# A fused recurrence, gated convolution and MLP on one core: two full rings of raw q/k/f tiles, a third activation buffer, three weights loaded in column halves, state copies on either of two engines, and another search for the order of the units

## The chip, the core and the metric

The kernel runs on one core of a Trainium2 chip. The metric is the device time of one execution in microseconds (us). TensorE (PE in the rows) does the matrix products and the transposes by an identity, VectorE (DVE), ScalarE (ACT) and GpSimd (POOL) the elementwise work, and SyncE (SP) issues every transfer. Each engine works through its own list of instructions in the order in which the program holds them.

## What is computed

All inputs are float32 numbers in four batches of 768 tokens; the weights come as float64 words and are turned into float32 on the chip. A recurrence per head gives y, a gated convolution with two products follows, and then a normalised two-layer MLP with a residual:

```python
def _attn_ref(q, k, v, f_logit):                     # 4 batches, 8 heads, 768 tokens, 48 wide
    f = 1.0 / (1.0 + np.exp(-f_logit))
    for t in range(S):
        state = f[:, :, t, :, None] * state + np.einsum('bhd,bhe->bhde', k[:, :, t], v[:, :, t])
        y[:, :, t] = np.einsum('bhd,bhde->bhe', q[:, :, t], state)

def _moe_ref(x, w_val, conv_w, w_out):               # x: 768 tokens x 384; conv_w: 5 x 384
    for k in range(K):
        gate_pre += conv_w[k][None, None, :] * xp[:, k:k + S, :]
    gate = 1.0 / (1.0 + np.exp(-gate_pre))
    return (gate * (x @ w_val) @ w_out)

def _moe2_ref(x, g_ln, w_ch1, w_ch2):                # w_ch1: 384 x 1536, w_ch2: 1536 x 384
    xn = (x - mu) / np.sqrt(var + 1e-06) * g_ln
    return x + np.maximum(xn @ w_ch1, 0.0) @ w_ch2
```

## The kernel before, in words

**Tiles and stages.** The 3072 tokens are worked in 24 tiles of 128 tokens, and two tiles make one of 12 groups of 256. A tile goes through the recurrence in chunks of 64 tokens: `load` and `load_v` bring q, k, f and v, `prep` turns f, k and q so that the channel lies on the partitions (`turned`) and makes the decays, scaled keys `kt` and scaled queries `mv` on DVE, `at_t` turns `kt` (PE block T) and copies it to `kn` on ACT, `at_a` makes the products inside a chunk (block A), `at_d` the state (block D, then `sd` on POOL, the copies `st<-sd` on ACT and `sn` on DVE), `at_y` the outputs (block Y) and copies them to `xt`, six small transfers on SP moving the last 16 rows of each head. A group then goes through `gates` (a product and four multiply-adds per 128 channels, the multiply-adds on DVE, and a sigmoid), `val` (27 matmuls on `wv`, `gt`), `x1` (18 on `wo`, then mean and variance, `rs` and `nb` on POOL, `xn` on ACT and its product with `gln`), `xnt` (the transposes `ps<-ident,xn`) and 6 steps of `c1` (18 matmuls and the relu) and `c2` (12 matmuls). Every product of these is done three times on parts: each operand is split into a high part `hi` and a rest `lo` of type float32r (`split`, `mm3`). The relu of `c1` leaves `hidden_hi` (ACT) and `hidden_lo` (DVE), which `c2` reads, from a ring of two buffers.

**The raw tiles.** The first eight tiles (`TURNED`) are loaded as they lie and turned by PE; from the ninth on they are loaded in four pieces and turned by DVE (`dve_transpose`). There is one set of full buffers `raw_f`, `raw_k`, `raw_q`, and a smaller set `odd_*` that only the odd ones of the first eight tiles use. `load(a + 1)` is written behind `prep(a)`.

**The weights.** They come through `stage`, four slots of 384 words of 8 bytes; `w_val` and `w_out` fill three slots each with transfers that cover 48 and 16 partitions (`ROWS`), `w_ch1` and `w_ch2` fill one slot at a time. `convert` puts a float32 together from the two halves of a float64 in four instructions for 128x384 words: one on POOL or ACT (`scaled`), one on ACT or DVE (`shifted`), one on ACT (`REBIAS`), one on DVE; `split` then makes `w_hi` (ACT or DVE) and `w_lo` (POOL or DVE).

**What sets the order.** The program is first recorded as units with their dependencies and a price on each engine that may do them; a planner (`schedule`, `pass_over`) then walks through them in modelled time, always taking the unit that can start first, by rank among equals. It also chooses the engine where there is a choice (`side` is POOL or DVE, `mover` ACT or DVE, `scaler` POOL or ACT; `BIAS` is added to DVE's side) and the PSUM bank of each result (8 banks, `ps`). 120 passes are made with ranks from a backward pass or with random shifts, and the one with the shortest modelled span is issued by `emit`, so that nearly every instruction has the line of one call in it (L413 before, L466 after). Groups 0 and 1 share the first halves of the MLP, so that each weight is used for both: steps 1 to 12 of `c1` belong to these two groups, the 13th opens group 2.

Of the kernel before, what the change touches and what calls it, by code (L numbers as in the profile page):

```python
# [21 lines left out]
DM = H * D  # L22
# [12 lines left out]
KS = 5  # L35
EPS = 1e-6
MIN_DECAY = 1e-15
PASSES = 120
ALTERNATE = 8
SPREADS = (0.5, 2.0, 6.0)  # L40
SEED = 1
# [4 lines left out]
load6 gates1 v5 w  # L46
# [5 lines left out]
BIAS = 0.9  # L52
# [8 lines left out]
SLOTS = 4  # L61

# [32 lines left out]
class Unit:  # L95


    def __init__(self, engine):
        self.costs = dict.fromkeys(engine.split("|"), 0.0)
        self.engine = next(iter(self.costs))  # L100
        self.calls = []
        self.delay = 0.0
        self.deps = set()
        self.opens = None
        self.uses = set()
        self.port = False
# [13 lines left out]
class Plan:  # L120
# [111 lines left out]
    def price(self, engine, method, out, ins, n, args, kw):  # L232
        if engine == "tensor":
            if method == "transpose":
                return 0.105 * self.slow
            if ins[0].dtype == F32R:
                return (0.436e-3 * n + 0.006) * self.slow
            return (0.056 if n > D else 0.043) * self.slow
        if engine == "scalar":
            scaled = sum(isinstance(kw.get(k), bass.AP) for k in ("scale", "bias"))  # L240
            part = 0.1 if out.ap[0][1] < 128 else 0.0
            return n / 1200 + (0.066 if ins[0].space == PSUM else 0.096) + 0.093 * scaled + part
        if engine == "vector":
            if method == "reciprocal":
# [12 lines left out]
            return n / (1920 if fast else 960) + 0.069 + 0.062 * scalars  # L257
        if engine == "gpsimd":
            if args and args[-1] == ALU.pow:
                return 0.5  # L260
            if method == "affine_select":
                return 0.62
            if method in ("memset", "tensor_copy"):
                return 0.0009 * n + 0.07
            return (0.0029 if method in ("tensor_scalar", "scaled") else 0.0024) * n + 0.1
        raise ValueError(engine)

    def transfer(self, issued, u, out, in_):

        n = size = mybir.dt.size(out.dtype)  # L270
        for _, k in out.ap:
            n *= k
        run = size * min(out.ap[-1][1], in_.ap[-1][1])
        local = out.space == in_.space
        issued.costs = {"sync": 0.63 if out.ap[0][1] == 64 or local else 0.47}
        issued.delay = 0.5
        u.costs = {"wire": n / run * (10.0 + (0.054 if run < 1024 else 0.048 if run < 2048 else 0.064) * run) / 16e3}
        u.delay = 1.2
        u.deps.add(len(self.units) - 1)

    def wait(self, u, v):

        if u.engine != v.engine:
            after = {"tensor": 0.17, "vector": 0.085, "scalar": 0.1, "gpsimd": 0.05}
            before = {"tensor": 0.07, "gpsimd": 0.085}
            return u.delay + after.get(u.engine, 0.05) + before.get(v.engine, 0.04)
        return u.delay + {"tensor": 0.0, "vector": 0.115, "scalar": 0.12}.get(u.engine, 0.11)

    def pass_over(self, deps, users, rank, wait, forward):
# [4 lines left out]
        free, waiting = {}, {}  # L294
# [6 lines left out]
        for u in units:  # L301
            for e in u.costs:
                free[e], waiting[e] = 0.0, []

        def enter(i):
            for e in units[i].costs if forward else [units[i].engine]:
                waiting[e].append(i)

        def start(i, e):
            t = max(free[e], ready[i])  # L310
            if units[i].port and e in port:
                t = max(t, port[other[e]])
            if forward and units[i].opens is not None:
                t = max(t, min(banks.values()) if banks else 1e9)
            if forward and units[i].opens is not None and e == "vector":
                t = max(t, sorted(banks.values())[1] if len(banks) > 1 else 1e9)
            if e == "sync":
                t = max(t, free["wire"] - BACKLOG)
            return t
# [4 lines left out]
        def fits(i, e):  # L324
            costs = units[i].costs
            return len(costs) == 1 or not forward or finish(i, e) <= min(finish(i, x) for x in costs)

        for i in range(len(units)):
            if not left[i]:
                enter(i)  # L330
        order = []
        while len(order) < len(units):
            best = None
            for e, q in waiting.items():
                for i in q:
                    t = (start(i, e), rank[i])
# [3 lines left out]
            if t >= 1e9:  # L340
                return None, None, 1e9, None
            u = units[i]
            for x in u.costs if forward else [e]:
                waiting[x].remove(i)
            u.engine = e
            order.append(i)
            end[i] = free[e] = t + u.costs[e]
            if u.port and e in port:
                port[e] = end[i] + 0.05
            if forward:  # L350
                if u.opens is not None:
                    homes[u.opens] = min(banks, key=banks.get)
                    del banks[homes[u.opens]]
                for r in u.uses:
                    held[r] -= 1
                    ends[r] = max(ends[r], end[i] + 0.17)
                    if not held[r]:
                        banks[homes[r]] = ends[r]
            for j in users[i]:
                left[j] -= 1  # L360
                ready[j] = max(ready[j], end[i] + wait(u, units[j]))
                if not left[j]:
                    enter(j)
        return order, end, max(free.values()), homes

    def schedule(self):

# [6 lines left out]
        back = lambda u, v: self.wait(v, u)  # L374
        draw = random.Random(SEED)
        rank, best, kept = list(range(len(units))), None, None
        for n in range(PASSES):
            order, end, span, homes = self.pass_over(deps, users, rank, self.wait, True)
            better = best is None or span < best[1]
            if better:  # L380
                best = order, span, [u.engine for u in units], homes
                kept = rank
            if order and (n < ALTERNATE or better):
                _, end, _, _ = self.pass_over(users, deps, [-t for t in end], back, False)
                rank = [-t for t in end]
            else:
                far = draw.choice(SPREADS)
                rank = [t + draw.gauss(0.0, far) for t in kept]
        order, self.makespan, engines, homes = best
# [26 lines left out]
class Kernel:  # L416
    def __init__(self, ctx, tc, aps):
# [29 lines left out]
        self.raw = {n: one(f"raw_{n}", [128, NP, 4 * D]) for n in "fkq"}  # L447
        self.odd = {n: one(f"odd_{n}", [128, N]) for n in "fkq"}
# [26 lines left out]
        self.hidden = [parts(f"hidden{i}", [128, 2, G]) for i in range(2)]  # L475
        self.banks = ring("ps", BANKS, [128, 512], pool=ps)

    def constants(self):
        nc = self.nc
        self.ns = self.n1 = self.n2 = self.na = self.nw = self.slot = 0  # L480
        for n, pad in (("f", 8.0), ("k", 0.0), ("q", 0.0)):
            for raw in (self.raw[n], self.odd[n]):
                nc.gpsimd.memset(self.by_token(raw)[:, :, D:], pad)
            nc.gpsimd.memset(self.raw[n][:, :, 160:192], pad)
# [272 lines left out]
    def at_d(self, a):  # L757
# [16 lines left out]
        for c in range(NC):  # L774
# [8 lines left out]
            else:  # L783
# [131 lines left out]
    def c1(self, g, i):  # L915
# [10 lines left out]
        hh, hl = self.hidden[self.n1 % 2]  # L926
# [4 lines left out]
    def c2(self, g, i, stops=(NK // 2 - 1,)):  # L931

        nc = self.nc
        hid = self.hidden[self.n2 % 2]
# [34 lines left out]
    def record(self):  # L969
# [205 lines left out]
```

## Time and profile before

| | us |
|---|---|
| median of 3 runs | 556.89 (556.07 to 557.33) |
| the profiled execution | 557.31 |
| its span | 555.6 |
| PE busy | 504.9 (91%) |
| DVE busy | 349.0 (63%) |
| ACT busy | 298.3 (54%) |
| POOL busy | 189.8 (34%) |

The span is the time between the first and the last recorded work of the profiled execution; its own time is 1.7 us longer. Busy shares are means over stages that differ: at the beginning weights and eight tiles come in and are converted, in the middle one group of 256 tokens follows another, and at the end a check of the decays and the last output follow.

### The profile page before, as it was taken

Reading aid. Unit: us, or ns where it says so; the run is one execution under the profiler, and the core shown is the slowest. Engines: PE = TensorE matmul, PEld = TensorE weight load, DVE = VectorE, ACT = ScalarE, POOL = GpSimd, SP = SyncE. Lnnn points to the kernel's source line nnn. Section 1 sums busy time; section 2 is a strip of 40 time slices with the busy share of each in tenths; the row PEclk is TensorE's granted clock in tenths of the full one; section 3 lists DMA queues with packets and bytes.
Section 4 is the critical chain, followed back from the end, with each engine's and each line's share of the span. In section 5 each row is a group of like instructions: output and inputs, shape, how many; then the busy total and the mean of one; then the engine's idle time right before and its main releaser. Section 6 shows DMA issues by size and latency. Waiting matters only on the chain.

```text
span 555.6 us, 13472 instructions
## 1 busy us (share of the span) xinstructions
PE 504.9 (91%) x5272; PEld 476.2 (86%) x5272; DVE 349.0 (63%) x681; ACT 298.3 (54%) x659; POOL 189.8 (34%) x298
## 2 busy tenths in 40 slices
PE   5656859999989999989989999999999999999994
PEld 4545749889989989989989989989989999999994
DVE  8737895589986686676676676676676361362311
ACT  4848999995464464464464464464463472421310
POOL 2433578763340341340440441430430541411200
PEclk9965979999999999999999999999999999999998
DMA  7996766542732332242232242242220010000000
GB/s 140 171 164 157 178 162 198 154 132 47 180 94 59 81 102 54 69 103 58 63 106 56 64 115 58 53 117 56 53 66 15 14 32 9 8 31 1 28 1 34
DMA packets 92128, 45.60 MB, mean 82 GB/s; under 512 B 56213, under 2 KB 89749, under 8 KB 92058
## 3 DMA queue, kind: packets, MB, share of 16 engines
q1 hardware_dynamic: 92058, 44.67, 34.3%
q8 instruction: 43, 0.70, 0.5%
q14 instruction: 27, 0.22, 0.1%
HBM read 38.75 MB, written 4.72 MB: 78 GB/s over the span
## 4 chain that ended last, share of the span: by engine, by line
PE 61%; ACT 14%; DVE 11%; DMA 5%; issue 4%; SPq 2%; POOL 2%; DVEq 0%; ACTq 0%; POOLq 0%
PE ps L413 61%; DVE ps L413 6%; ACT wt L413 4%; ACT ps L413 3%; DMA raw_f<-in_f_logit 3%; SPq L413 2%; DMA xt<-x 2%; ACT w_hi L413 1%; DVE x L413 1%; POOL rs L413 1%; ACT st L413 1%; ACT x L413 1%; DVE hidden_lo L413 1%; DVE ps L961 1%; ACT kn L413 1%
## 5 line engine op out<-in xcount | busy, mean ns | idle before, releaser
L413 PE MATMUL ps<-nh,w_hi 128*128 128x256 f32 x432 | 124.4, 288 | 0.2 <-ACT nh L413 0.2
L413 PE MATMUL ps<-nl,w_hi 128*128 128x256 f32 x432 | 120.5, 279 | 0.3 <-DVE nl L413 0.2
L413 PE MATMUL ps<-nh,w_lo 128*128 128x256 f32 x432 | 120.3, 279 | 0.0
L413 PE MATMUL ps<-w_hi,hidden_hi 128*128 128x384 f32 x288 | 100.8, 350 | 0.1
L413 PE MATMUL ps<-w_hi,hidden_lo 128*128 128x384 f32 x288 | 97.1, 337 | 0.1
L413 DVE SCALAR_TENSOR_TENSOR hidden_lo<-ps,hidden_hi 128x512 fp32r<-128x512 f32 x72 | 49.3, 685 | 76.0 <-ACT hidden_hi L413 75.9
L413 PE MATMUL ps<-w_lo,hidden_hi 128*128 128x384 f32 x288 | 96.8, 336 | 0.0
L413 PEld LDWEIGHTS ps<-nh,w_hi 128*128 128x128 f32 x432 | 81.2, 188 | 2.0 <-ACT nh L413 0.4
L413 PEld LDWEIGHTS ps<-nl,w_hi 128*128 128x128 f32 x432 | 81.2, 188 | 0.7 <-DVE nl L413 0.7
L413 PEld LDWEIGHTS ps<-nh,w_lo 128*128 128x128 f32 x432 | 81.7, 189 | 0.0
L413 ACT ACTIVATE hidden_hi<-ps 128x512 fp32r<-128x512 f32 x72 | 43.0, 597 | 59.5 <-PE ps L413 59.3
L413 DVE SCALAR_TENSOR_TENSOR ps<-xt,convw,ps 128x256 f32<-128x256 f32 x144 | 66.1, 486 | 12.5 <-ACT ps L413 10.6
L413 POOL TENSOR_TENSOR gl<-gt,gh 128x512 fp32r<-128x512 f32 (+1 forms) x24 | 24.3, 1014 | 108.5 <-ACT gh L413 108.5
L413 PEld LDWEIGHTS ps<-w_hi,hidden_hi 128*128 128x128 f32 x288 | 54.1, 188 | 2.4 <-ACT hidden_hi L413 0.4
L413 PEld LDWEIGHTS ps<-w_hi,hidden_lo 128*128 128x128 f32 x288 | 54.1, 188 | 0.5 <-DVE hidden_lo L413 0.4
L413 PEld LDWEIGHTS ps<-w_lo,hidden_hi 128*128 128x128 f32 x288 | 54.2, 188 | 0.0
L413 ACT COPY st<-sd 48x192 f32<-48x192 f32 x88 | 31.0, 353 | 40.7 <-POOL sd L413 39.3
L413 POOL TENSOR_SCALAR_AFFINE_SELECT mv<-mv 64x512 f32<-64x512 f32 x48 | 31.6, 658 | 50.5 <-ACT mv L413 48.6
L413 POOL TENSOR_TENSOR sd<-sn,fc 112x192 f32<-112x192 f32 x44 | 22.5, 510 | 55.1 <-DVE sn L413 45.7
L413 PEld LDWEIGHTS ps<-mv,st 112*48 112x48 f32 (+1 forms) x768 | 24.5, 126 | 15.4 <-ACT st L413 9.2
L413 PE MATMUL ps<-mv,st 112*48 112x64 f32 (+1 forms) x768 | 29.1, 225 | 9.0 <-ACT st L413 8.0
L413 ACT COPY kn<-ps 64x192 f32<-64x192 f32 x96 | 30.2, 315 | 9.9 <-PE ps L413 8.8
(105 smaller groups left out, 1032.4 us busy)
## 6 DMA issues: line engine op xcount, KB each, us to landing
stage<-in_moe_w_ch SPq DMA_DIRECT2D x24, 384.0 KB, 4.0
st<-in_v SPq DMA_DIRECT2D x96, 48.0 KB, 2.5
out_x<-x SPq DMA_DIRECT2D x24, 192.0 KB, 1.9
raw_f<-in_f_logit SPq DMA_DIRECT2D x32, 96.0 KB, 2.4
raw_k<-in_k SPq DMA_DIRECT2D x32, 96.0 KB, 2.2
raw_q<-in_q SPq DMA_DIRECT2D x32, 96.0 KB, 2.4
raw_f<-in_f_logit SPq DMA_DIRECT2D x32, 80.0 KB, 2.3
raw_k<-in_k SPq DMA_DIRECT2D x32, 80.0 KB, 2.2
```

Source lines behind the costliest of these rows:

```text
L413: getattr(getattr(self.nc, engine), method)(*args, **kw)
L961: self.tc.nc.vector.memset(t, 0.0)
```

## The change

- `raw` becomes a list of two whole sets, tile `a` uses set `a % 2` throughout, and `load(a + 2)` is written behind `prep(a)`.
- `hidden` has three buffers (`RING`).
- `w_val` and `w_out` (`load_rows`) and `w_ch2` (`weight_2`) are loaded in two halves of 192 columns each; a transfer of `w_ch2` now covers 256 rows of 192 columns, in place of 128 rows of 384.
- The copies `st<-sd` may be done by POOL or ACT, as the planner chooses.
- The planner has other prices and constants (`BIAS` 0.3 in place of 0.9, `MARGIN` on what follows a load, at most `FLIGHT` transfers under way, dearer bytes), 8 passes without random shifts, and then a table `MOVED` of 47 entries that shift the ranks of runs of units; its first line is shown. A scratch area of the compiler's for transfers from POOL is cut to 1024 bytes; the kernel has no such transfers.

```diff
-PASSES = 120
...
+PASSES = 8
...
-BIAS = 0.9
+BIAS = 0.3
...
+RING = 3
+MARGIN = 2.5
+FLIGHT = 8
+
+MOVED = (
+    (416, 8, -12), (2566, 20, -8), (22, 6, 5), (1533, 20, -20), (1524, 40, 8), (1231, 3, 8),
...
+                if len(sent) >= FLIGHT:
+                    last = end[sent[-FLIGHT]]
+                    t = max(t, last + 1.2) if last else NEVER
...
+        if MOVED:
+            rank = list(kept)
+            for first, n, by in MOVED:
+                for i in range(first, first + n):
+                    rank[i] += by
+            best = self.forward(deps, users, rank)
...
-        self.raw = {n: one(f"raw_{n}", [128, NP, 4 * D]) for n in "fkq"}
-        self.odd = {n: one(f"odd_{n}", [128, N]) for n in "fkq"}
+        self.raw = [{n: one(f"raw{i}_{n}", [128, NP, 4 * D]) for n in "fkq"} for i in range(2)]
...
-        self.hidden = [parts(f"hidden{i}", [128, 2, G]) for i in range(2)]
+        self.hidden = [parts(f"hidden{i}", [128, 2, G]) for i in range(RING)]
...
-        for r, m, c, step in ROWS:
-            self.nc.sync.dma_start(
-                out=words[r : r + m].rearrange("p (j n) -> p j n", j=NJ),
-                in_=w[c : c + NJ * step].rearrange("(j r) n -> r j n", r=step)[0:m],
-            )
+        for n in (slice(0, HALF), slice(HALF, DM)):
+            for r, m, c, step in ROWS:
+                self.nc.sync.dma_start(
+                    out=words[r : r + m].rearrange("p (j n) -> p j n", j=NJ)[:, :, n],
+                    in_=w[c : c + NJ * step].rearrange("(j r) n -> r j n", r=step)[0:m, :, n],
+                )
...
-        for u in range(2):
+        for n in (slice(0, HALF), slice(HALF, DM)):
             words = self.slots(1)
-            f0 = 256 * i + 128 * u
-            self.nc.sync.dma_start(out=words, in_=self.w_ch2[f0 : f0 + 128])
-            self.split([t[:, u] for t in self.w2[i]], self.convert(words))
+            self.nc.sync.dma_start(
+                out=words.rearrange("p (u n) -> p u n", u=2),
+                in_=self.w_ch2[256 * i : 256 * i + 256].rearrange("(u r) n -> r u n", u=2)[:, :, n],
+            )
+            w = self.convert(words).rearrange("p (u n) -> p u n", u=2)
+            self.split([t[:, :, n] for t in self.w2[i]], w)
...
-        return self.odd if a < TURNED and a % 2 else self.raw
+        return self.raw[a % 2]
...
-                    nc.scalar.copy(st[o : o + D, hh, c], sd[o : o + D])
+                    self.scaler().copy(st[o : o + D, hh, c], sd[o : o + D])
...
-                if 1 < a + 1 < NT:
-                    self.load(a + 1)
+                if a + 2 < NT:
+                    self.load(a + 2)
```

The order moves on every engine. Three places are shown.

On SP, around the first six transfers `xt<-x` (without which no `gates` of group 0 can start), stood before all of `w_out` (384 columns wide), a slot of `w_ch1` and three raw tiles ahead of v and of those six:

```order
L413 DMA st_112<-in_v 64x4x48 x4
L413 DMA stage<-in_moe_w_out 48x3x384
L413 DMA stage<-in_moe_w_out 16x3x384
L413 DMA stage<-in_moe_w_out 48x3x384
L413 DMA stage<-in_moe_w_out 16x3x384
L413 DMA stage<-in_moe_w_ch 128x3x128
L413 DMA raw_k<-in_k 128x8x48
L413 DMA raw_q<-in_q 128x8x48
L413 DMA odd_f<-in_f_logit 128x8x48
L413 DMA st_113<-in_v 64x4x48 x2
L413 DMA xt_128<-x_127 16x256 x6
```

Now only the first column half of `w_out`, the slot of `w_ch1` and one raw tile stand there, behind the whole of v, and the second half of `w_out` follows after the six:

```order
L466 DMA st_113<-in_v 64x4x48 x4
L466 DMA stage<-in_moe_w_out 48x3x192
L466 DMA stage<-in_moe_w_out 16x3x192
L466 DMA stage<-in_moe_w_out 48x3x192
L466 DMA stage<-in_moe_w_out 16x3x192
L466 DMA stage<-in_moe_w_ch 128x3x128
L466 DMA raw_k<-in_k 128x8x48
L466 DMA xt_128<-x_127 16x256 x6
L466 DMA raw_f<-in_f_logit 128x8x48
L466 DMA raw_q<-in_q 128x8x48
L466 DMA stage<-in_moe_w_out 48x3x192
```

Of the words that stand ahead of these six transfers in the whole list of SP, 6.90 MB before and 6.60 MB now come out of the shapes. At the head of SP's list, four transfers of v and two pieces of `w_val` now stand ahead of the first `raw_f`, which was the third transfer before and is the seventh now.

On DVE, behind the conversion of the first slot of `w_out` and the first weights of the MLP, stood before, up to the first `hidden_lo`:

```order
L413 TENSOR_TENSOR kt_116<-ps_161,gs 128x512
L413 TENSOR_TENSOR nl_149<-ps_158,nh_147 128x3x128
L413 SCALAR_TENSOR_TENSOR wt<-ps_162,wt 128x384
L413 TENSOR_SCALAR lows<-gs 128x8
L413 TENSOR_TENSOR fc_119<-gs,ps_159 128x8
L413 RECIPROCAL starts<-lows 128x8
L413 SCALAR_TENSOR_TENSOR wt<-ps_155,wt 128x384
L413 TENSOR_TENSOR gt<-gt,ps_157 128x512
L413 SCALAR_TENSOR_TENSOR ft<-ps_159,starts 128x512
L413 SCALAR_TENSOR_TENSOR wt<-ps_158,wt 128x384
L413 SCALAR_TENSOR_TENSOR hidden_lo<-ps_161,hidden_hi 128x512
```

Now casts to `w_hi`, the rests `w_lo`, the part `wt<-stage` of a conversion and the product of `xn` with `gln` stand among them:

```order
L466 SCALAR_TENSOR_TENSOR wt<-ps_161,wt 128x384
L466 BN_STATS bns_138<-x_135 128x6
L466 CAST w_0_hi<-wt 128x2x192
L466 BN_AGGR bna_140<-bns_138 128x2
L466 CAST w_0_hi<-wt 128x3x128
L466 TENSOR_TENSOR w_0_lo<-wt,w_0_hi 128x2x192
L466 TENSOR_SCALAR wt<-stage 128x384
L466 TENSOR_TENSOR w_0_lo<-wt,w_0_hi 128x3x128
L466 TENSOR_TENSOR xn_145<-xn_145,gln 128x384
```

Ahead of the thirteenth `hidden_lo` of DVE's list stand now, more than before: 9 casts to `w_hi`, 10 `wt<-stage`, 8 `w_lo`, 3 `xn<-xn,gln`, one `xl`, one `gl`, one `sd`, two `sn`, one `gs`, one `kt` and one `gt`. No kind stands there less often.

On POOL, at the first state updates, stood before:

```order
L413 AFFINE_SELECT mv_114<-mv_114 64x512 x2
L413 TENSOR_TENSOR sd_126<-sn_124,fc_119 112x192
L413 TENSOR_TENSOR sd_125<-sn_123,fc_120 112x192
L413 TENSOR_SCALAR wt<-stage 128x384
L413 AFFINE_SELECT mv_115<-mv_115 64x512 x2
```

Now copies to `st` stand behind each `sd` (one half of them or both), which ACT did before:

```order
L466 TENSOR_TENSOR sd_126<-sn_124,fc_119 112x192
L466 COPY st_112<-sd_126 48x192
L466 TENSOR_TENSOR sd_125<-sn_123,fc_120 112x192
L466 AFFINE_SELECT mv_114<-mv_114 64x512 x2
L466 COPY st_113<-sd_125 48x192 x2
L466 TENSOR_TENSOR sd_126<-sn_124,fc_120 112x192
L466 COPY st_113<-sd_126 48x192
```

In the whole program, ACT gives away 50 of the 88 copies to `st` (to POOL), 8 of its parts `wt<-stage`, 9 casts to `w_hi` and one of two table loads. PE has the same instructions as before in another order: ahead of the matmuls of `c2` that read the thirteenth `hidden_lo` stand 18 more matmuls of `val` and one block more of each of T, A and D.

## Rows read from the trace of the kernel before

**Rows 1.** The page, busy time, share of the span and instructions of TensorE.

```profile
PE 504.9 (91%) x5272; PEld 476.2 (86%) x5272; DVE 349.0 (63%) x681; ACT 298.3 (54%) x659; POOL 189.8 (34%) x298
```

**Rows 2.** Windows (from:to, length, PE PEld DVE ACT POOL, clock, DMA, GB/s).

```profile
0.00:42.60 42.60, 23.74 (x339) 19.41 (x339) 27.07 (x54) 25.30 (x58) 14.96 (x40) 0.89 0.90 159
42.60:167.30 124.70, 107.81 (x1134) 99.75 (x1135) 100.57 (x200) 103.25 (x232) 69.54 (x90) 0.93 0.56 144
...
125.00:138.90 13.90, 13.27 (x148) 12.53 (x147) 13.61 (x28) 8.25 (x21) 4.83 (x5) 1.00 0.24 47
167.30:555.60 388.30, 373.40 (x3801) 357.09 (x3799) 221.36 (x427) 169.77 (x372) 105.27 (x168) 0.99 0.22 54
```

**Rows 3.** What TensorE waited for up to 168.5 us: total, times, longest.

```profile
PE ps L413 <- ACT st L413: 8.0, 2, 7.2
PE ps L413 <- DMA raw_f<-in_f_logit: 7.6, 2, 5.3
PE ps L413 <- DVE wt L413: 3.9, 1, 3.9
PE ps L413 <- DVE mv L413: 3.6, 3, 2.8
```

**Rows 4.** Timeline of SyncE's queue, 29 to 47 us: start, length, transfers.

```profile
29.86 1.97 SPq L413 DMA_DIRECT2D stage<-in_moe_w_out  x4
...
34.14 6.41 SPq L413 DMA_DIRECT2D odd_f<-in_f_logit  x1
...
42.63 3.78 SPq L413 DMA_DIRECT2D xt<-x  x6
```

**Rows 5.** Timeline of ScalarE there; the idle time before a row is in brackets.

```profile
40.23 1.36 ACT L413 ACTIVATE ps<-stage 128x384 f32<-128x384 f32 x3 [7.40 <-DMA stage<-in_moe_w_out]
```

**Rows 6.** What TensorE waited for from 168.5 us on.

```profile
PE ps L413 <- ACT gt L413: 6.8, 6, 1.4
```

**Rows 7.** Groups by form: count, total busy us, mean ns, idle time before.

```profile
L413 DVE CAST w_hi<-wt 128x384 fp32r<-128x384 f32 x1 | 0.5, 544 | 0.0
L413 DVE TENSOR_SCALAR wt<-stage 128x384 uint16<-128x384 uint16 x3 | 1.4, 474 | 0.0
L413 DVE TENSOR_TENSOR x<-x,ps 128x384 f32<-128x384 f32 x28 | 15.3, 548 | 2.8 <-PE ps L413 2.8
L413 DVE TENSOR_TENSOR_SCAN gs<-ps,ends 128x511 f32<-128x511 f32 x24 | 29.2, 1218 | 3.8 <-ACT ps L413 3.1
L413 DVE TENSOR_TENSOR kt<-ps,gs 128x512 f32<-128x512 f32 x24 | 16.4, 685 | 2.9 <-PE ps L413 2.8
L413 ACT COPY st<-sd 48x192 f32<-48x192 f32 x88 | 31.0, 353 | 40.7 <-POOL sd L413 39.3
L413 POOL TENSOR_TENSOR sd<-sn,fc 112x192 f32<-112x192 f32 x44 | 22.5, 510 | 55.1 <-DVE sn L413 45.7 <-DVE fc L413 6.8 <-DVE lows L413 2.5
```

**Rows 8.** Timeline of GpSimd and VectorE at 35 us.

```profile
35.01 0.66 POOL L413 TENSOR_SCALAR_AFFINE_SELECT mv<-mv 64x512 f32<-64x512 f32 x1
...
35.24 0.45 DVE L413 TENSOR_SCALAR lows<-gs 128x8 f32<-128x8 f32 x1
```

**Rows 9.** Timeline: first and last of 18 `val`; a block A; thirteenth `c2`.

```profile
53.45 0.37 PE L413 MATMUL ps<-xh,wv_hi 128*128 128x256 f32 x1
...
55.47 0.28 PE L413 MATMUL ps<-xh,wv_lo 128*128 128x256 f32 x1
...
163.26 1.15 PE L413 MATMUL ps<-mv,kt 48*64 48x64 f32 x32
...
167.34 0.69 DVE L413 SCALAR_TENSOR_TENSOR hidden_lo<-ps,hidden_hi 128x512 fp32r<-128x512 f32 x1 [1.56 <-ACT hidden_hi L413]
...
168.55 0.33 PE L413 MATMUL ps<-w_hi,hidden_hi 128*128 128x384 f32 x1
```

**Rows 10.** Timeline from 231 us: copy of `x1`, and the product with `gln`.

```profile
231.83 0.48 ACT L413 COPY x<-ps 128x384 f32<-128x384 f32 x1 [0.90 <-PE ps L413]
...
235.70 1.03 POOL L413 TENSOR_TENSOR xn<-xn,gln 128x384 f32<-128x384 f32 x1 [0.83 <-ACT xn L413]
```

More of the change, by code (lines that the diff above doesn't have):

```diff
@@ L293, in pass_over @@
         end = [0.0] * len(units)
-        free, waiting = {}, {}
+        free = dict.fromkeys(ENGINES, 0.0)
+        waiting = {e: [] for e in ENGINES}
+        sent = []
         port = {"vector": 0.0, "gpsimd": 0.0}
@@ L300, in pass_over @@
         ends = [0.0] * len(held)
[L301 to L307, printed above, removed]
         def start(i, e):
+            u = units[i]
             t = max(free[e], ready[i])
-            if units[i].port and e in port:
+            if u.port and e in port:
                 t = max(t, port[other[e]])
[L313 to L316, printed above, removed]
+            if u.opens is not None:
+                first = sorted(banks.values())
+                spare = 1 if e == "vector" else 0
+                t = max(t, first[spare]) if len(first) > spare else NEVER
             if e == "sync":
                 t = max(t, free["wire"] - BACKLOG)
+                if len(sent) >= FLIGHT:
+                    last = end[sent[-FLIGHT]]
+                    t = max(t, last + 1.2) if last else NEVER
             return t
@@ L325, in fits @@
             costs = units[i].costs
-            return len(costs) == 1 or not forward or finish(i, e) <= min(finish(i, x) for x in costs)
-        for i in range(len(units)):
+            return len(costs) == 1 or all(finish(i, e) <= finish(i, x) for x in costs)
+        for i, u in enumerate(units):
             if not left[i]:
-                enter(i)
+                for e in u.costs:
+                    waiting[e].append(i)
         order = []
@@ L333, in pass_over @@
             best = None
-            for e, q in waiting.items():
-                for i in q:
-                    t = (start(i, e), rank[i])
+            for e in ENGINES:
+                for i in waiting[e]:
+                    t = (start(i, e), ready[i] if e == "wire" else rank[i])
                     if (best is None or t < best[0]) and fits(i, e):
@@ L339, in pass_over @@
             (t, _), i, e = best
-            if t >= 1e9:
-                return None, None, 1e9, None
+            if t >= NEVER:
+                return None
             u = units[i]
-            for x in u.costs if forward else [e]:
+            for x in u.costs:
                 waiting[x].remove(i)
@@ L347, in pass_over @@
             end[i] = free[e] = t + u.costs[e]
+            if e == "sync":
+                sent.append(i + 1)
             if u.port and e in port:
                 port[e] = end[i] + 0.05
[L350 to L358, printed above, removed]
+            if u.opens is not None:
+                homes[u.opens] = min(banks, key=banks.get)
+                del banks[homes[u.opens]]
+            for r in u.uses:
+                held[r] -= 1
+                ends[r] = max(ends[r], end[i] + 0.17)
+                if not held[r]:
+                    banks[homes[r]] = ends[r]
             for j in users[i]:
                 left[j] -= 1
-                ready[j] = max(ready[j], end[i] + wait(u, units[j]))
+                ready[j] = max(ready[j], end[i] + self.wait(u, units[j]))
                 if not left[j]:
-                    enter(j)
-        return order, end, max(free.values()), homes
+                    for x in units[j].costs:
+                        waiting[x].append(j)
+        return max(free.values()), order, [u.engine for u in units], homes, end
     def schedule(self):
@@ L373, in schedule @@
                 users[d].append(i)
[L374 to L389, printed above, removed]
+        rank, best = list(range(len(units))), None
+        for _ in range(PASSES):
+            got = self.forward(deps, users, rank)
+            if got is None:
+                break
+            if best is None or got[0] < best[0]:
+                best, kept = got, rank
+            rank = [-t for t in self.backward(deps, users, [-t for t in got[4]])]
+        if MOVED:
[4 more added lines that the diff above has]
+            best = self.forward(deps, users, rank)
+        self.deps, self.next, self.rank = deps, users, kept
+        self.makespan, order, engines, homes, self.ends = best
         return order, engines, homes
@@ L480, in constants @@
         self.ns = self.n1 = self.n2 = self.na = self.nw = self.slot = 0
[L481 to L484, printed above, removed]
+        for raws in self.raw:
+            for n, pad in (("f", 8.0), ("k", 0.0), ("q", 0.0)):
+                nc.gpsimd.memset(self.by_token(raws[n])[:, :, D:], pad)
+                nc.gpsimd.memset(raws[n][:, :, 160:192], pad)
         nc.gpsimd.memset(self.ends, 0.0)
@@ L933, in c2 @@
         nc = self.nc
-        hid = self.hidden[self.n2 % 2]
+        hid = self.hidden[self.n2 % RING]
         self.n2 += 1
```

60 lines of the change are left out of this document (47 added, 13 removed), and 7 rows, old and new, of the table MOVED.

## The prediction

> **What bounds the kernel now.** The page says that TensorE is busy for 504.9 us, 91% of the span [rows 1]. The other 50.7 us are what a change of order can reach, so I looked for where they lie. The windows [rows 2] answer that: up to 42.6 us TensorE works 23.74 us (idle 18.9), from there to 167.3 us it is idle for 16.9, and in the 388.3 us behind that for 14.9. The early stretch is a third of the span and has 35.8 of the 50.7 us.
>
> The waits of TensorE by releaser name what ended them. Up to 168.5 us [rows 3] the largest single ones are 7.2 us for a copy to `st`, 5.3 for the first raw tile, 3.9 for a converted weight and 2.8 for `mv`: four different releasers, so the reader is to see that no one engine is the bound there. The 7.2 us are a transfer in disguise. SP put `w_out` into its queue at 29.86 us, and the issue of one raw tile at 34.14 us took 6.41 us, where most take under 1; the six `xt<-x` behind it came only at 42.63 [rows 4]. ScalarE had meanwhile stood for 7.40 us before the first conversion of `w_out`, with the copies to `st` behind that row in its order [rows 5]. The DMA share is 0.90 in that stretch, and 0.56 and 0.22 behind it [rows 2]: transfers bound the first 43 us only.
>
> From 168.5 us on there is one wait worth a name, 6.8 us in six places for `gt` [rows 6]: the sigmoid of `gates` holds a PSUM bank that the second transpose of a group opens next. The rest of the idle time there is the end of the program (check and last output), which the change leaves alone.
>
> So the question has two parts: how early the thirteenth `c2` starts, the first one of the steady part (168.55 us, with `hidden_lo` ready at 167.34 + 0.69 [rows 9]), and what the 387.05 us behind it lose.
>
> **The change part by part.**
>
> *Transfers.* The bytes ahead of the first `xt<-x` fall from 6.90 to 6.60 MB. At the 159 GB/s of the first stretch [rows 2] those are 41.5 us, so these six can land at about 44 us as before; but half of `w_out` now comes behind them, and with it every conversion of `w_out` that could hold ScalarE's copies. I take the 7.2 us as gone from TensorE's list and do not add them as a gain: what is late next is VectorE, below. Two rings and the earlier `load` move issues, not bytes; after 42.6 us the DMA share covers them. If that cover were gone (share 0.9 again), the old stall of 7 us would come back. Halves keep bytes and conversions, and cost 12 issues more, 0.63 us each by the six of 3.78 us [rows 4], 7.6 us of SP's time that lies in a queue which waits more than it issues; I take nothing, with 7.6 as the other end. Four more transfers ahead of the first `raw_f` make the first tile 2.5 us later (4 x 0.63): VectorE starts its first scan at about 10 us, having done some 5 us of memsets, so it has lost 5.
>
> *Engines.* ScalarE loses 50 copies to `st` of 0.353 us [rows 7], 17.7 us, and some 10 more of conversions. On GpSimd such a copy is not in the trace: nothing is the lower end and 0.51 us of `sd`, which has two inputs of that width, the upper one [rows 7]; at 0.51 it is 25 us over the program, and GpSimd, busy for 84.5 of the first 167.3 us [rows 2], gives `w_lo` and products with `gln` away. I take it as covered. A copy that follows `sd` on its own engine is no further from the block Y than one on ScalarE.
>
> VectorE pays. Ahead of the thirteenth `hidden_lo` stand more: 9 casts x 0.544 = 4.9; 10 `wt<-stage` x 0.474 = 4.7; 15 instructions of at most 384 columns (8 `w_lo`, 3 `xn`, 2 `sn`, `sd`, `gl`) at the 0.548 of `x<-x,ps` = 8.2; `xl` as two of those, 1.1; `gs` 1.2; `kt` and `gt` 0.685 each, 1.4 [rows 7]. That is 21.5 us. Before it did 27.07 + 100.57 = 127.6 us up to 167.3 [rows 2]. So 149.1 us of work must now pass through VectorE ahead of that row.
>
> *When that is done.* This is the number that I cannot read: what share of its time VectorE then works. Over 42.6 to 167.3 us it was 100.57/124.7 = 0.81, with ScalarE at 103.25/124.7 = 0.83 beside it, each waiting for the other; where VectorE alone was pressed, 125.0 to 138.9 us, it was 13.61/13.9 = 0.98 [rows 2]. ScalarE and GpSimd both get lighter, so the case is nearer to the second; I take 0.92. Then `hidden_lo` thirteen is done at 5 + 149.1/0.92 = 167.1 us, and its `c2`, whose first two matmuls do not read it, starts at 166.8. At 0.98 that is 156.8, at 0.81 it is 188.8.
>
> *Behind it.* More of TensorE's work is then already done: 18 matmuls of `val`, 2.1 us from 53.45 to 55.47 + 0.12, a block A of about 1.1 [rows 9], and T and D, which are shorter; together 4.5. Of the 6.8 us for `gt` [rows 6] I take 4 as gone, between 0 and all: the transposes open other banks in most groups now. The third `hidden` buffer frees no wait that stands in the rows, so it is worth nothing by itself.
>
> *Sum.* 166.8 + 387.05 - 4.5 - 4 = 545.4 us of span against 555.6. The profiled execution took 557.31 us, 1.7 more than its span, and lies 0.4 above the median of 556.89. 545.4 + 1.7 = **547 us**.
>
> **A rule against it.** In one place the two engines visibly stood in each other's way: the small `lows` of VectorE, 8 columns, started at 35.24 us and took 0.45 us, ending 0.02 us after a select on GpSimd that had begun at 35.01 and took 0.66 [rows 8]. The Trainium skill, "GPSIMD Engine Reference", section 8 (Key points), says that GpSimd shares its SBUF interfaces with VectorE and that they collide when VectorE runs a two-port mode or reads two SBUF inputs. By that rule the trace agrees. As a mechanism of this kernel: of the instructions that VectorE gains, 33 (casts, `wt<-stage`, `w_lo`, `xn`, `xl`, `gl`, `sd`) read SBUF alone. GpSimd was busy for 84.5/167.3 = 0.51 of the time; a held instruction waits for half of an operation, 0.3 to 0.5 us by rows of 0.51 to 1.03 [rows 7, 10]: 33 x 0.51 x 0.42 = 7 us, which brings the forecast from 547 to 554.
>
> **The rivals.**
>
> 1. *VectorE packs tightly* (0.97 to 0.98 as in its best stretch). For it: fewer cross waits, since a conversion that VectorE does itself needs no word from ScalarE. Against: even when pressed it followed others at chunk edges. 156.8 + 378.55 + 1.7 = **537**.
>
> 2. *VectorE becomes a bound that costs more than was won* (the other side). Place: ahead of `hidden_lo` thirteen; the 21.5 us added, with holds as above. It decides from the share at which `c2` thirteen starts at 177.05 us (168.55 + 8.5): 149.1/172.4 = 0.865. For it: 0.81 was the mean so far, and the holds of the rule alone bring 0.92 down to 0.88. Against: the mean was made while ScalarE was as full. At 0.84: 182.2 + 378.55 + 1.7 = **562**.
>
> 3. *The gain is given back in the middle.* The new order has stretches in which the front ends of two groups stand side by side on TensorE with little `c1` between. From the copy of `x1` to the end of the product with `gln` 4.9 us pass (231.83 to 236.73 [rows 10]); where `val`, Y and D do not fill them, the transpose waits. Three places of 3 us: 547 + 9 = **556**, no difference. For it: the `gt` waits show that the steady part has little slack. Against: 4 us of other blocks stand between in the places that I saw.
>
> 4. *The transfers do as before*: with 41.5 us of bytes ahead of `xt<-x` the stall would move instead of going, 547 + 7 = **554**. I count it within the upper part of the forecast's own range.
>
> **How the numbers follow.** Forecast 0.42 (shares 0.89 to 0.95: 542 to 553; of this 0.10 for the holds of the rule, at 554), rival 1 0.20, rival 2 0.22, rival 3 0.16. A difference below 0.2%, 1.1 us, cannot be told from no change here. Faster by more: 0.42 + 0.20 + half of rival 3 = 0.70; within: 0.08; slower: 0.22. The range reaches into both outer cases, down to 536 and up to 561, leaving out about 0.05 below and 0.12 above.
>
> **What would show it.** The thirteenth `hidden_lo` on VectorE at 160 to 173 us, and VectorE busy for 145 to 152 us ahead of it; ScalarE no longer near full; no issue on SP of several us ahead of the first `xt<-x`; TensorE's largest early waits released by VectorE (`kt`, `mv`, `wt`, `hidden_lo`) in place of `st`; the wait for `gt` below 4 us. Wrong would be: a thirteenth `c2` behind 177 us; small VectorE instructions that end together with GpSimd's rows in many places (the rule); or a list of waits behind that row that has grown beyond 10 us (rival 3).

## The result, and the profile after

The changed kernel takes 538.15 us (median of 4 runs, 536.39 to 539.33) against 556.84 for the kernel before: a ratio of 0.9663, 95% interval 0.9631 to 0.9695. The profiled execution took 538.87 us with a span of 537.2. So 18.7 us were gained where 9.9 were forecast (547): within the range of 536 to 561 but near its lower end, and close to the time of rival 1 (537). In the later sets of runs the kernel before took 557.06 to 558.25 us; each ratio below is to the kernel before in the same set, while differences of medians across sets can be off by as much.

The page of the changed kernel, busy time by engine (against [rows 1]), then its windows (columns as in [rows 2]), up to the thirteenth `hidden_lo` at 158.48 us, and from the thirteenth `c2` at 159.48:

```profile
PE 501.3 (93%) x5272; PEld 477.9 (89%) x5272; DVE 369.1 (69%) x737; ACT 270.6 (50%) x591; POOL 169.5 (32%) x312
```

```profile
0.00:42.60 42.60, 28.92 (x483) 24.01 (x485) 32.96 (x67) 25.41 (x61) 19.39 (x53) 1.00 0.79 156
42.60:158.48 115.88, 103.95 (x1087) 98.51 (x1082) 108.81 (x228) 93.45 (x202) 60.77 (x89) 0.97 0.65 167
0.00:158.48 158.48, 132.87 (x1562) 122.52 (x1563) 141.77 (x294) 118.87 (x262) 80.15 (x141) 0.98 0.69 164
159.48:537.20 377.72, 367.39 (x3704) 354.39 (x3702) 226.33 (x442) 151.75 (x329) 89.21 (x171) 0.99 0.21 51
```

TensorE's idle time falls from 50.7 to 35.9 us (537.2 - 501.3), its busy time by 3.6 with the same 5272 matmuls. The 18.4 us of span split at the thirteenth `c2` into 9.1 ahead (168.55 to 159.48) and 9.3 behind (387.05 to 377.72). In the first 42.6 us TensorE did 483 matmuls where it had done 339, at a granted clock of 1.00 in place of 0.89; in the next stretch the clock is 0.97 in place of 0.93.

What TensorE waited for in the changed kernel up to 159.2 us, by releaser (against [rows 3]):

```profile
PE ps L466 <- DMA raw_f<-in_f_logit: 8.8, 2, 8.4
PE ps L466 <- DVE kt L466: 5.1, 5, 1.8
PE ps L466 <- DMA raw_q<-in_q: 2.4, 2, 1.3
PE ps L466 <- DVE wt L466: 1.8, 1, 1.8
```

The same from 159.48 us on (against [rows 6]):

```profile
PE ps L466 <- DVE nl L466: 0.6, 2, 0.3
PE ps L466 <- DVE kt L466: 0.4, 1, 0.4
...
PE ps L466 <- DVE x L466: 0.3, 1, 0.3
PE ps L466 <- ACT gt L466: 0.2, 1, 0.2
```

The wait for `st` of 7.2 us is gone, VectorE's results are the commonest releasers, and the one large wait is the start, for the first raw tile (8.4 us, against 5.3 before). Behind the thirteenth `c2` no wait on work inside the pipeline reaches 1 us; the 6.8 us for `gt` are 0.2.

SyncE's queue of the changed kernel, from 18 us (against [rows 4]):

```profile
18.79 3.67 SPq L466 DMA_DIRECT2D raw_k<-in_k  x1
...
34.22 1.99 SPq L466 DMA_DIRECT2D stage<-in_moe_w_out  x4
...
38.84 4.36 SPq L466 DMA_DIRECT2D xt<-x  x6
```

The six `xt<-x` are issued 3.8 us earlier than before (38.84 against 42.63). One issue of 3.67 us is left, far ahead of them.

VectorE's and TensorE's timeline of the changed kernel at the thirteenth step (against [rows 9]):

```profile
155.21 0.14 DVE L466 TENSOR_TENSOR fc<-gs,ps 128x8 f32<-128x8 f32 x1
155.28 0.70 DVE L466 STREAM_TRANSPOSE ps<-raw_k 128x512 f32<-128x512 f32 x1
155.89 1.18 DVE L466 TENSOR_TENSOR_SCAN gs<-ps,ends 128x511 f32<-128x511 f32 x1
...
158.48 0.69 DVE L466 SCALAR_TENSOR_TENSOR hidden_lo<-ps,hidden_hi 128x512 fp32r<-128x512 f32 x1 [0.61 <-ACT hidden_hi L466]
...
159.48 0.34 PE L466 MATMUL ps<-w_hi,hidden_hi 128*128 128x384 f32 x1
```

Look at the first three rows: 155.21 + 0.14 is 0.07 behind the start of the next, 155.28 + 0.70 is 0.09 behind the start of the third. Here a queued row starts before the one ahead of it has ended, so durations of rows add up to more than the time that they fill.

The groups of the changed kernel (against [rows 7]):

```profile
L466 POOL COPY st<-sd 48x192 f32<-48x192 f32 x50 | 17.8, 356 | 5.7 <-DVE sd L466 3.1
L466 DVE CAST w_hi<-wt 128x384 fp32r<-128x384 f32 x10 | 4.7, 467 | 0.0
L466 DVE TENSOR_SCALAR wt<-stage 128x384 uint16<-128x384 uint16 x13 | 6.4, 492 | 0.1
L466 DVE TENSOR_TENSOR w_lo<-wt,w_hi 128x384 fp32r<-128x384 f32 x8 | 4.4, 546 | 0.0
```

### The profile page after: what moved, and what is told of

Read it like the earlier page. It is cut to its first block, busy times and chain, and to the rows that moved or that the text cites. A ratio compares the mean times of both kernels' runs of the same rounds, so it can differ in the third digit from the quotient of the medians.

```text
span 537.2 us, 13413 instructions
## 1 busy us (share of the span) xinstructions
PE 501.3 (93%) x5272; PEld 477.9 (89%) x5272; DVE 369.1 (69%) x737; ACT 270.6 (50%) x591; POOL 169.5 (32%) x312
## 4 chain that ended last, share of the span: by engine, by line
PE 71%; DVE 12%; DMA 4%; POOL 4%; ACT 3%; issue 2%; SPq 2%; DVEq 0%; POOLq 0%; ACTq 0%
PE ps L466 71%; DVE ps L466 4%; SPq L466 2%; POOL rs L466 2%; DVE mv L466 2%; DMA raw_q<-in_q 1%; DVE wt L466 1%; DMA xt<-x 1%; DMA stage<-in_moe_w_ch 1%; DVE gs L466 1%; ACT xn L466 1%; DVE bns L466 1%; DMA raw_f<-in_f_logit 1%; DMA out_x<-x 1%; DVE nl L466 1%
## 5 line engine op out<-in xcount | busy, mean ns | idle before, releaser
L466 PE MATMUL ps<-w_hi,hidden_hi 128*128 128x384 f32 x288 | 99.3, 345 | 0.0
L466 ACT COPY kn<-ps 64x192 f32<-64x192 f32 x96 | 30.1, 313 | 14.1 <-PE ps L466 12.9
L466 DVE TENSOR_TENSOR_SCAN gs<-ps,ends 128x511 f32<-128x511 f32 x24 | 29.1, 1214 | 9.3 <-ACT ps L466 8.9
L466 DVE TENSOR_TENSOR mv<-ps,ft 64x512 f32<-64x512 f32 x48 | 33.0, 688 | 2.5 <-PE ps L466 1.0
L466 PE MATMUL ps<-xh,wv_hi 128*128 128x256 f32 x108 | 32.7, 302 | 0.9 <-DVE gt L466 0.9
L466 PE MATMUL ps<-xl,wv_hi 128*128 128x256 f32 x108 | 31.4, 291 | 0.0
```

The lines of the kernel that those rows point to most:

```text
L466: getattr(getattr(self.nc, engine), method)(*args, **kw)
```

## The experiments

**One thing alone, or all but the table.** In the first, `MOVED` is emptied. In the second, moreover, all parts of the kernel before are put back under the new planner; in the third the planner of before orders the new parts.

```diff
-MOVED = (
-    (416, 8, -12), (2566, 20, -8), (22, 6, 5), (1533, 20, -20), (1524, 40, 8), (1231, 3, 8),
...
+MOVED = ()
```

> The changed kernel without its table MOVED; rings, third buffer, halves, copies to st on either engine and the new prices stay. Its order has 4.54 MB instead of 6.50 MB ahead of the first xt<-x, and on VectorE, ahead of the thirteenth hidden_lo, one gs, kt, gt and sd less, 6 conversions less and two gl more, some 5 us less work. Theory A (the new prices and the parts make the gain, the table only trims): 538 to 543 us, thirteenth c2 at 157 to 163 us, waits for gt under 2 us. Theory B (the table made the order that packs): 546 to 552 us, with waits for gt of 4 us or more behind the thirteenth c2.

> The new planner with its prices but no table, on the parts of the kernel before: one raw ring with the small odd one, two hidden buffers, whole-width w_val, w_out and w_ch2, copies to st on ScalarE alone. Theory A (the order is what counts, above all that VectorE takes conversions from ScalarE): 541 to 547 us, no several-us wait of TensorE for st. Theory B (the parts count): 551 to 557 us, with a wait of several us for st or for w_out left in the first 45 us.

> The parts without the planner: two raw rings, three hidden buffers, halves, copies to st on either engine, ordered by the planner of before with its 120 passes and its BIAS of 0.9. On VectorE ahead of the thirteenth hidden_lo it has no more conversions than before; 48 copies to st are on GpSimd. Theory A: 550 to 557 us, waits for gt of 5 us or more remain. Theory B: 540 to 548 us, thirteenth c2 before 163 us.

Measured: without the table 551.78 us (ratio to before 0.9885, 0.9843 to 0.9926); planner alone 562.49 (1.0076, 1.0051 to 1.0102); parts alone 568.45 (1.0177, 1.0132 to 1.0222). Theory B holds for the table, by its time. For the two halves apart neither theory does: each alone is slower than before, and only together do they gain 5.1 us by medians and 6.4 by the ratio. TensorE's two largest sums of waits by releaser over the whole span, of the planner alone (the 7.5 us are its start), then of the parts alone:

```profile
PE ps L457 <- ACT kn L457: 10.0, 5, 4.5
PE ps L457 <- DVE xn L457: 7.5, 1, 7.5
```

```profile
PE ps L415 <- ACT gt L415: 13.0, 7, 3.3
PE ps L415 <- DVE wt L415: 8.0, 5, 4.3
```

And of the kernel without a table, behind its thirteenth `c2` (161.25 us), with one of the five places:

```profile
PE ps L457 <- DVE x L457: 7.6, 5, 2.1
PE ps L457 <- ACT kn L457: 1.4, 1, 1.4
```

```profile
361.20 1.15 PE L457 MATMUL ps<-mv,kt 48*64 48x64 f32 x32 [2.09 <-DVE x L457]
```

No `gt` there any more, as expected of theory A, but a block A now waits for the bank that `x<-x,ps` frees at the end of a group: the wait had changed its place, not gone. Its stretch behind the thirteenth `c2` takes 549.3 - 161.25 = 388.05 us, as before (387.05). The two raw rings, the column halves and the planner's new constants were not put back one by one, so what each of them is worth stays open.

**The table in two parts**, the 22 entries of units ahead of the thirteenth `hidden_lo` alone, and the 25 others alone.

```diff
 MOVED = (
-    (416, 8, -12), (2566, 20, -8), (22, 6, 5), (1533, 20, -20), (1524, 40, 8), (1231, 3, 8),
+    (416, 8, -12), (22, 6, 5), (838, 1, 1), (613, 6, -20), (842, 20, 2), (725, 3, 3),
...
```

> Only the 22 entries of the table that shift units ahead of the thirteenth hidden_lo; the order up to there is that of the changed kernel, behind it the ranks are unshifted. Theory A (two separate gains: the early entries pack the first stretch, the late ones take away the waits for PSUM banks): thirteenth c2 at 159 to 160, then 6 us or more of waits for the bank of x<-x,ps or for gt, 543 to 547 us. Rival (the early stretch carries the later one along: more front-end work done ahead leaves the slack): waits behind it below 3 us, 538 to 541 us.

> Only the 25 entries that shift units from the thirteenth hidden_lo on; ahead of it the order is that without a table. Theory A: thirteenth c2 at 161 to 162, waits behind it below 3 us, 542 to 546 us. Rival: the waits behind it stay at 8 us or more, 548 to 552 us.

Measured: early entries 546.72 us (0.9798, 0.9757 to 0.9839), late entries 542.30 (0.9728, 0.9687 to 0.9770). Theory A by both times and both lists of waits: the two gains are separate and add up. From 551.78 the early entries save 5.1 us alone and 4.1 beside the late ones; the late ones 9.5 and 8.6. The thirteenth `c2` came at 157.35 and 159.16, earlier than the 159 to 160 and 161 to 162 expected. One and the same order up to there gave 161.25 (no table) and 159.16 (late entries), another one 159.48 (the changed kernel) and 157.35 (early entries): profiled executions differ there by some 2 us, and how much of the early entries' gain lies ahead of that point is not settled. TensorE's waits behind the thirteenth `c2`, early entries alone, then late ones alone:

```profile
PE ps L462 <- DVE x L462: 7.6, 5, 2.1
PE ps L462 <- ACT kn L462: 1.4, 1, 1.4
```

```profile
PE ps L463 <- DVE nl L463: 0.6, 2, 0.3
PE ps L463 <- DVE x L463: 0.5, 2, 0.3
```

**The copies to `st`** back on ScalarE, in the changed kernel's order.

```diff
         for method, args, kw in u.calls:
+            if method == "copy" and set(u.costs) == {"gpsimd", "scalar"}:
+                engine = "scalar"
```

> The changed kernel, same order on every engine, but all 88 copies st<-sd on ScalarE again: 50 x 0.351 = 17.6 us back on ScalarE, some 9 of it ahead of the thirteenth c2, 17.8 us off GpSimd. Theory A (VectorE's list sets when the thirteenth c2 starts, ScalarE is only filled to 0.75): 537 to 541 us, thirteenth c2 within 2 us of 159.5. Rival (ScalarE's relief is what was needed): 545 to 550 us, thirteenth c2 at 166 or later, and waits of TensorE for st of 3 us or more.

Measured: 538.06 us (0.9640, 0.9609 to 0.9671), thirteenth `c2` at 158.72: theory A. The window up to its thirteenth `hidden_lo`:

```profile
0.00:157.72 157.72, 134.71 (x1562) 123.45 (x1563) 141.01 (x294) 124.32 (x281) 73.48 (x122) 0.97 0.68 165
```

To move the 50 copies from ScalarE to GpSimd is worth nothing that can be measured. The run changes both engines at once, ScalarE gets more and GpSimd less, so it does not show by itself that neither matters; but VectorE is as busy ahead of the thirteenth `hidden_lo` (141.01 us against 141.77).

**A dose on either engine.** The other kernel has a copy of 128x384 on ScalarE in place of the memset.

```diff
+            if self.units[i].calls and self.units[i].calls[0][0] == "reciprocal" and tiles < 10:
+                tiles += 1
+                for _ in range(2):
+                    self.nc.vector.memset(ker.spare, 0.0)
```

> The changed kernel, same order, with 20 memsets of 128x512 on VectorE into a tile that nobody reads, two behind each of the first ten reciprocals (starts), all ahead of the thirteenth hidden_lo. By the row of the memset (485 ns) they are 9.7 us, by the overlap of queued rows (0.05 to 0.09 us each) 8 to 8.7. Theory A (VectorE's list sets when the thirteenth c2 starts): thirteenth c2 at 167 to 169 us, 545.5 to 548 us in all. Rival (VectorE's 16.7 us of idle time ahead of it take most of them, TensorE's own list or the start sets it): thirteenth c2 at 160 to 163.5, 538.5 to 542 us.

> The same with 20 copies of 128x384 on ScalarE into that tile at the same places, about 20 x 0.48 = 9.6 us by the rows of such copies. Theory A: ScalarE is idle for 39.6 of the first 158.5 us and takes them in, thirteenth c2 at 159 to 162, 538 to 541 us. Rival (ScalarE is on the path as much as VectorE): thirteenth c2 at 165 or later, 544 us or more.

Measured: 545.48 us on VectorE (0.9780, 0.9736 to 0.9824), 540.25 on ScalarE (0.9683, 0.9640 to 0.9726). Group and window up to the thirteenth `hidden_lo` of the dose on VectorE, then of that on ScalarE:

```profile
L452 DVE MEMSET spare<- 128x512 f32 x20 | 9.7, 485 | 2.3 <-DVE spare L452 1.6 <-ACT ps L471 0.2
```

```profile
0.00:164.19 164.19, 135.03 (x1562) 124.04 (x1563) 149.74 (x314) 119.25 (x262) 80.14 (x141) 0.96 0.65 158
```

```profile
0.00:160.07 160.07, 133.93 (x1562) 121.73 (x1563) 142.06 (x293) 127.72 (x282) 80.23 (x141) 0.98 0.66 163
```

9.7 us of rows fill 149.74 - 141.77 = 8.0 us of VectorE; the thirteenth `hidden_lo` comes 5.7 us later, its `c2` at 165.19, between the ranges of the two theories, and the median rises by 7.3 to just under theory A's range. 127.72 - 118.87 = 8.9 us on ScalarE move `hidden_lo` by 1.6 and the median by 2.1, with the thirteenth `c2` at 161.07: theory A there, and the 1.6 us are no more than the 2 us by which executions differ. VectorE's list is the nearer bound, by 0.71 against 0.18 us for each us added. Of the 5.7 us 2.2 are TensorE's own busy time (135.03 against 132.87), at a granted clock of 0.96 in place of 0.98.

**The start.** The first `raw_f`, or the three raw pieces of the first tile, at the head of SP's list.

```diff
+        head = list(dict.fromkeys(head))
...
+        return head + [i for i in order if i not in head]
```

> The changed kernel with the first raw_f moved from the seventh to the first place of SP's list, where it is issued at about 1.8 us instead of 4.90; nothing else moves. Theory A (the late first tile is 2.5 us that VectorE loses, and VectorE sets the thirteenth c2): first scan at 7.3 to 7.8 us instead of 10.17, thirteenth c2 at 157 to 158, 535.3 to 536.3 us. Rival (the first raw_k, raw_q or the next tile is late instead, and the gain is gone by 40 us): first scan as early, but thirteenth c2 within 0.7 us of 159.5, 537.5 to 538.6 us.

> As the kernel with the first raw_f ahead, but raw_f, raw_k and raw_q of the first tile all stand at the head of SP's list. Theory A (VectorE's list sets the thirteenth c2, and the 3.6 us that TensorE then waited for the first raw_k are the next loss): second scan at 12 to 13.5 us instead of 15.65, thirteenth c2 at 155 to 157, 533.5 to 536 us. Rival (v or w_val is late in its place, or the gain is taken in by VectorE's idle time later): thirteenth c2 at 157.5 or later, 536.5 to 538.5 us.

Measured: 537.31 us (0.9631, 0.9589 to 0.9674) and 536.67 (0.9622, 0.9589 to 0.9655). The first two scans (`gs`) of the second one:

```profile
6.49 1.22 DVE L466 TENSOR_TENSOR_SCAN gs<-ps,ends 128x511 f32<-128x511 f32 x1 [0.33 <-ACT ps L466]
...
14.43 1.19 DVE L466 TENSOR_TENSOR_SCAN gs<-ps,ends 128x511 f32<-128x511 f32 x1
```

With the whole tile ahead the first scan is 3.7 us earlier than in the changed kernel, the second only 1.2. The thirteenth `c2` is 2.2 us earlier with the first `raw_f` ahead (157.29) and 2.8 with the whole tile (156.70). Both medians are lower than the changed kernel's, but their intervals overlap its interval, and profiled executions with one and the same early order differ there by some 2 us, as above. Neither theory is shown; if there is a gain, it is some 1 to 2 us.

**Two `hidden` buffers**, planned anew with the same ranks, and in the changed kernel's own order, where an instruction moves back only if it must.

```diff
+        global RING
+        RING = 2
...
+            i = next(i for i in left if deps[i] <= done and (units[i].opens is None or free))
```

> The changed kernel with two hidden buffers instead of three; every unit keeps its rank, so the order changes only where the third buffer is missed. Theory A (the third buffer frees no wait that shows): 537 to 540 us, no new wait of more than 1 us. Rival (the order found needs it, since c1 runs two steps ahead of c2 in places): 543 us or more, with TensorE waiting for hidden_hi or hidden_lo.

> Two hidden buffers again, but this time in the changed kernel's own order, on its engines: an instruction moves back only where the third buffer is missed, which is four relus to hidden_hi on ScalarE, two hidden_lo on VectorE and one c2 product of six matmuls on TensorE; banks keep their numbers where they are free. Theory A (the buffer by itself is worth little; the 7.7 us of the run with two buffers came from what the planner then arranged differently behind it): 537.5 to 540.5 us. Rival (the order needs the third buffer): 543 to 547 us, with TensorE waiting for hidden_hi, hidden_lo or gt for 4 us or more behind the thirteenth c2.

Measured: 545.87 us (0.9792, 0.9750 to 0.9834) and 546.69 (0.9791, 0.9770 to 0.9813). The rival holds by its times: the order needs the third buffer, which is worth 8.5 us in it by medians and 7.1 by the ratios. By its waits it holds less: behind the thirteenth `c2` those for `hidden_hi`, `hidden_lo` and `gt` come to 3.6 us in the same order, and with the order planned anew the largest are 2.8 for `gt`, 2.2 for `sn` and 1.9 for `nl`. The profiled execution in the same order has a span longer by 9.3 us (546.5 against 537.2); 5.5 of them lie behind the thirteenth `c2`, 4.2 as idle time (14.5 us, against 10.3):

```profile
163.27:546.47 383.19, 368.69 (x3704) 354.11 (x3702) 226.64 (x442) 151.83 (x329) 89.26 (x171) 0.99 0.20 50
```

The other 3.8 lie ahead of it, where they are seen on TensorE's timeline and windows, with two buffers in the same order, then in the changed kernel:

```profile
149.00 0.90 PE L466 MATMUL ps<-ident,xn 128*128 128x128 f32 x3 [2.29 <-DVE xn L466]
```

```profile
149.00:155.50 6.50, 6.50 (x54) 6.10 (x55) 4.92 (x10) 4.59 (x13) 2.32 (x3) 0.50 0.59 164
```

```profile
148.07 0.55 PE L466 MATMUL ps<-ident,xn 128*128 128x128 f32 x3 [0.98 <-DVE xn L466]
```

```profile
149.00:155.50 6.50, 6.50 (x125) 6.05 (x125) 6.35 (x15) 5.59 (x15) 2.90 (x6) 1.00 0.55 152
```

The same transposes wait for 2.29 us in place of 0.98, and behind them TensorE works at a granted clock of 0.50, its level of 1.2 GHz, for the 6.5 us shown: busy throughout, 54 matmuls in place of 125. So in this place a wait longer by 1.3 us costs, as an estimate, 3 us more behind it (half of the 6.5). That the missing buffer caused it is not shown: with the order planned anew the thirteenth `c2` came at 158.58, earlier than with three buffers, and one execution in the same order had a mean granted clock of 0.993, against 0.990 in the changed kernel, and still took 545.23 us.

Nor does the length of a wait alone decide what the clock does. Two waits of the run with the early entries alone, each with a window of the `c1` matmuls behind it:

```profile
189.04 1.15 PE L462 MATMUL ps<-mv,kt 48*64 48x64 f32 x32 [1.38 <-ACT kn L462]
190.60:193.80 3.20, 3.20 (x17) 3.20 (x16) 1.51 (x3) 1.37 (x3) 1.31 (x2) 0.50 0.63 188
```

```profile
232.26 1.15 PE L462 MATMUL ps<-mv,kt 48*64 48x64 f32 x32 [1.83 <-DVE x L462]
233.40:236.60 3.20, 3.20 (x28) 3.20 (x28) 1.53 (x3) 2.34 (x4) 1.31 (x2) 1.00 0.81 221
```

Behind the shorter one, 1.38 us, the granted clock is 0.50, behind the longer one, 1.83 us, it is 1.00.

## Why the prediction was right, and where it was off

**The sum.** It made the span from the start of the thirteenth `c2` (166.8 us forecast, 159.48 measured) and the stretch behind it (378.55 forecast, 377.72 measured). Of the miss of 8.2 us of span (545.4 against 537.2) 7.3 are in the first. The prediction's own signs for that point were missed on the low side, both by a little: the thirteenth `hidden_lo` at 158.48 us where 160 to 173 was given, and VectorE busy for 141.77 us ahead of it where 145 to 152 was given.

**The mis-sized term: the 21.5 us that VectorE was to gain.** The instructions were counted rightly but for one `fc` of 0.15 us, and by rows of the changed kernel up to 158.48 us they last 20.0 us. All rows ahead of that point last 18.7 us more than before (158.7 against 140.0), but VectorE is busy for only 14.1 us more (141.77 against 127.6). The step added durations to a busy time, and some 0.08 us of a queued row lies under the next. Ahead of the thirteenth `hidden_lo` 146 of 254 rows of VectorE started under the one before them, and the rows overlapped by 12.3 us in all; now it is 210 of 293 rows and 17.0 us: 4.6 us of what the step missed. The dose shows the same: 9.7 us of rows, 8.0 us of VectorE. The Trainium skill, "Perfetto Trace Analysis", section "Optimizing Scalar/DVE Operations", says that part of a profiled latency overlaps with the next instruction; the rows here agree.

**The share of 0.92** is what was measured: 141.77/(158.48 - 5) = 0.924. It had been chosen between 0.81 and 0.98, with a reason for the side but none for the figure, so that it came out so closely is luck. The forecast's own formula with the measured work gives 5 + 141.8/0.92 = 159.1. So rival 1's time came, but not by its mechanism (0.97 to 0.98): there was less to pack. That VectorE is what mainly sets this point is shown by the two doses; that it alone does is not, since 0.29 of the dose was taken in. Why VectorE could work so closely is not taken apart: without the table the thirteenth `c2` came at 161.25 already, and the planner and the parts were each slower alone.

**Transfers.** The stall of 7.2 us went, as forecast (rival 4 fell), and the first scan came at 10.17 us for "about 10". Not foreseen: `xt<-x` came 3.8 us earlier, and an issue of 3.67 us stayed. Two figures were wrong without weight in the sum: the lists of SP hold 442 transfers before and 450 now, so the halves cost 8 issues more and not 12, and what stands ahead of the first `xt<-x` is 6.80 MB before and 6.50 MB now by the sizes of the transfers; 6.90 and 6.60 hold the six themselves.

**ScalarE and GpSimd.** The copies cost 0.356 us on GpSimd, between the bounds, and are covered; putting them back on ScalarE leaves the time as it was.

**The rule against it** (holds between GpSimd and VectorE, 7 us) did not show in that size: with 17.8 us less on GpSimd VectorE's busy time stayed within 0.8 us. In the trace of the changed kernel two rows of VectorE are over 0.15 us longer than the median of their kind while GpSimd works, by 1.5 us together. One is a `gl` at 413.49 us, the other this `wt<-stage`, 1.65 us against a median of 0.39:

```profile
66.95 1.84 POOL L466 TENSOR_TENSOR xl<-xt,xh 128x768 fp32r<-128x768 f32 x1
67.40 1.65 DVE L466 TENSOR_SCALAR wt<-stage 128x384 uint16<-128x384 uint16 x1
```

**Behind the thirteenth `c2`** 4.5 us of moved work were forecast and TensorE's busy time there fell by 4.8 (372.15, which is 387.05 less its 14.9 of idle time, to 367.39); 4 us of waits were to go, and the idle time fell by 4.6 (14.9 to 10.3). The size was right, in part by luck. The reason was thin: no part of the change takes the bank waits away by itself, only together with the late entries of the table do they go. And the third buffer, put at nothing, is in it: without it, in the same order, the stretch takes 383.19 us. Rival 3, gain given back in the middle, is false for the changed kernel. Without the late entries its size comes (9 us in six places), but not by its mechanism: the waits are a block A's for a bank, not a transpose's for `xn`.

**The third buffer at nothing** was wrong. Next to no wait of TensorE in the rows of before would be freed by it (0.6 us for `hidden_lo`), and there the order had been made for two. In the new order it is worth 7.1 to 8.5 us.

**Left out of the sum: the clock.** 3.6 us of the 18.4 are TensorE's own busy time. It waits less, and less of its work is done at 1.2 GHz: up to 42.6 us the granted clock is 1.00 in place of 0.89, and in the next stretch 0.97 in place of 0.93 ([rows 2] against the windows above).

## What to carry to other kernels

Do not add the durations of rows to a busy time of an engine that is packed: take what a queued row adds, by the starts of its neighbours. In this kernel a buffer's worth could not be read from the trace of an order that was made without it; ask instead whether the new order has producers that run further ahead. And count with a wait of TensorE the stretch at the lower clock that may follow it.

## What had not been expected of the hardware

Behind one wait of 2.29 us in a stretch that was otherwise full the granted clock was 0.50 for the 6.5 us shown; behind one of 0.98 us at the same place it was 1.00. Elsewhere a wait of 1.38 us was followed by 0.50 and one of 1.83 us was not. A float32 copy of 48x192 takes as long on GpSimd (0.356 us) as on ScalarE (0.351).
